# Two up-weight loads moved to ScalarE's queue, the parameter rows moved to SyncE's

## The chip, the cores and the metric

The kernel runs on one core of a Trainium2 chip. Its engines work side by side: TensorE (PE in the profile; its weight loads are shown as PEld), VectorE (DVE), ScalarE (ACT), GpSimd (POOL) and SyncE (SP). Each engine takes its instructions in the order written and waits for others through semaphores. DMA transfers are issued here from the queues of SyncE and of ScalarE; the profile calls the issuing instructions SPq and ACTq. The metric is the time in microseconds (us) of one execution on the device. Less is better.

## The reference

The input x has 2048 rows of 512 numbers. Every row is normalised, and the normalised rows go through two branches that are added to x.

```python
xn = _layernorm(x, axis=-1)
return x + _A_ref(xn, ...) + _B_ref(xn, ...)

def _A_ref(x, Lambda_re, Lambda_im, B_re, B_im, C_re, C_im, log_dt, Dskip):
    dt = jnp.exp(log_dt)
    Lam_bar = jnp.exp(dt * Lam)
    B_bar = ((Lam_bar - 1.0) / Lam)[:, None] * Bmat
    Bu = jnp.einsum("bld,pd->blp", x + 0j, B_bar)
    # for every t: h = Lam_bar * h + Bu[:, t]
    y = 2.0 * jnp.einsum("blp,dp->bld", hseq, Cmat).real + x * Dskip

def _B_ref(x, w_gate, w_up, w_down):
    return (_gelu(x @ w_gate) * (x @ w_up)) @ w_down
```

The first branch is a state space layer with 512 complex states; log_dt, Lambda_re and Lambda_im are its parameter rows, 512 numbers each. The second is a gated feed-forward layer: w_gate and w_up are 512 x 1376, w_down is 1376 x 512. Inputs, weights and the output are bfloat16.

## The kernel before

The 2048 rows are worked in four blocks of 512, and a block is four tiles of 128 rows. For a block the kernel makes the normalised rows, transposes them by DMA so that the 512 features lie on the partitions, multiplies them with the gate and up weights, gates the products, multiplies with the state space input matrix, scans over time on VectorE, and gathers both branches in the output matmuls. TensorE has matmuls of some block to do through nearly the whole run.

The start is arranged differently, and it is the start that the change touches. For block 0 the rows of x are only centred (mean subtracted), transposed on TensorE (`cent_T`, L684) and copied out by ScalarE (L689); the division by the standard deviation is applied to the results. The gate and up products of tiles 0, 1 and 2 over the first 512 hidden columns are built up while the weights arrive: the 512 features are four *steps* k = 0 to 3 of 128, and `GT_k` (L701) adds one step's product to the sum in PSUM. Each step has a load of its own for the gate weights and for the up weights (`ld_wk`, L488, 128 x 512, 128 KB). So TensorE needs, in this order: the gate weights of step 0, the up weights of step 0 (each for tiles 0 and 1), the same for step 1, then gate and up of step 2; then tile 2 catches up on steps 0 to 2, and step 3 closes the sums of all three tiles. After that `GT_mm` (L712) does tile 3 and the columns 512 to 895 of all four tiles, for which the weights come in two larger loads of 384 KB (`ld_w` with slice 1, L493). Two more loads of 480 KB (slice 2, `load_W`) hold the columns from 896 on.

The parameter rows are three loads of 1 KB (`load_par`, L510), each into four rows of a small tile PROW that GpSimd has set to zero (L477). When all three have landed, SyncE issues one DMA transpose of that tile (`tr_par`, L515), which puts the parameters on the partitions. GpSimd's power (L557) and then VectorE's table work (from L558) start from it. On SyncE's queue the transposes of block 0's normalised rows follow (`TR(0)`, L736, four, each waiting for VectorE's L634), then tile loads of block 1 (L482), two long DMA transposes of B_re and B_im (L526), the load of Dskip (L535), x of block 2 (L482), and the transposes of block 1 (`TR(1)`, L736 again), which the matmuls `BU(1)` (L749) read.

What sets the order: a planner inside the kernel. Every operation is written down with an engine, a duration estimated by a formula, and what it reads and writes. For TensorE and SyncE the order is the order in which the operations are written. For ScalarE, VectorE and GpSimd the planner plays the program through with its own durations, and chooses among what is ready by priority. A DMA costs it 0.5 us of the issuing queue, then 2 us plus the bytes at a fixed rate, one transfer after the other. `S.order_behind(op, prev)` pins an operation behind another of the same engine without a semaphore; `GATE["par"]` holds the last DMA of such a chain on ScalarE's queue, and the mean of tile 1 (L956), ScalarE's first computing step, stands behind the chain's end.

The loads at the start go out in this order. SyncE: x tile 0, then for every step its gate and its up weights, with x tile 3 ahead of step 3, then slice 1 of both, slice 2 of both, and tr_par. ScalarE: x tile 1, the three parameter rows, x tile 2.

Of the kernel before, what the change touches and what calls it, by code (L numbers as in the profile page):

```python
# [365 lines left out]
def build(nc, ins, out):  # L366
    with ExitStack() as es:
        E = es.enter_context
        S = Sched(nc, es)
# [9 lines left out]
        WG = A.alloc("WG", [KD, F], BF16)  # L379
        WU = A.alloc("WU", [KD, F], BF16)  # L380
# [4 lines left out]
        WGc = [Buf("WGc%d" % i, "sbx", 10 * i, 10 * i + 1) for i in range(KD + 2)]  # L385
        WUc = [Buf("WUc%d" % i, "sbx", 100 + 10 * i, 101 + 10 * i) for i in range(KD + 2)]
# [34 lines left out]
        PROW = A.alloc("PROW", [128], BF16)  # L421
        PROW16 = Buf("PROW16", "sb", PROW.lo, PROW.hi, PROW.ap[0:16, :])
        PROWq = [Buf("PROW%d" % q, "prow", q, q + 1) for q in range(3)]
# [46 lines left out]
        GATE = {"before_gelu": [], "nh": 0}  # L470
        SCR = A.alloc("SCR", [1], F32)
        half = V(lambda e: e.memset(HALF.ap, 0.5), D_TINY, [], [HALF], "half")
# [10 lines left out]
                X_all.ap[:, 4 * b:4 * b + 4, :], x2[512 * b:512 * (b + 1), :].rearrange("(j p) d -> p j d", p=128)),  # L483
                512 * 1024, writes=X[4 * b:4 * b + 4], tag="ld_x%d" % b)

        def ld_wk(W, Wc, src, k):
            f0, f1 = FC[0]
            return S.dma(lambda e: e.dma_start(W.ap[:, k, f0:f1], src[128 * k:128 * (k + 1), f0:f1]),  # L488
                         256 * (f1 - f0), writes=[Wc[k]], tag="ld_w")

        def ld_w(W, Wc, src, n):
            f0, f1 = FC[n]
            return S.dma(lambda e: e.dma_start(W.ap[:, :, f0:f1], src[:, f0:f1].rearrange("(k p) f -> p k f", p=128)),  # L493
                         1024 * (f1 - f0), writes=[Wc[KD + n - 1]], tag="ld_w")

        def ld_x0(j, queue="sync", after=()):
            return S.dma(lambda e, j=j: e.dma_start(X[j].ap, x2[128 * j:128 * (j + 1), :]), 128 * 1024, writes=[X[j]], tag="ld_x0", queue=queue, after=after)  # L497
        ld_x0(0)
        GATE["par"] = S.order_behind(ld_x0(1, "scalar", [wrm]), GATE["table"])
        for k in range(KD):  # L500
            if k == 3:
                ld_x0(k)
            ld_wk(WG, WGc, ins["B_w_gate"], k)
            ld_wk(WU, WUc, ins["B_w_up"], k)
        ld_w(WG, WGc, ins["B_w_gate"], 1)
        ld_w(WU, WUc, ins["B_w_up"], 1)

        def load_par():
            for q, nm in enumerate(("A_log_dt", "A_Lambda_re", "A_Lambda_im")):
                GATE["par"] = S.order_behind(S.dma(lambda e, q=q, nm=nm: e.dma_start(PROW.ap[4 * q:4 * q + 4, :], ins[nm].rearrange("(s p) -> s p", p=128)),  # L510
                      1024, writes=[PROWq[q]], tag="ld_" + nm, queue="scalar", after=[half]), GATE["par"])
            GATE["par"] = S.order_behind(ld_x0(2, "scalar"), GATE["par"])

        def tr_par():
            S.dma(lambda e: e.dma_start_transpose(PAR.ap.rearrange("p q t -> p (q t)").unsqueeze(1), PROW16.ap), 4096,  # L515
# [434 lines left out]
        def sub(j):  # L950
            return V(lambda e: e.tensor_scalar(XN[j].ap, X[j].ap, MVt[0][j].ap[:, 0:1], None, ALU.subtract),
                     d_dve_ts4x(512), [X[j], MVt[0][j]], [XN[j]], "sub")
        load_par()
        load_W()
        tr_par()
# [103 lines left out]
def bass_parallel_sum__ssm_conv_s5__geglu_ffn__prompt_kernel(  # L1059
    nc: bass.Bass,  # L1060
    A_x: bass.AP,
    A_Lambda_re: bass.AP,
    A_Lambda_im: bass.AP,
    A_B_re: bass.AP,
    A_B_im: bass.AP,
    A_C_re: bass.AP,
    A_C_im: bass.AP,
    A_log_dt: bass.AP,
    A_Dskip: bass.AP,
    B_x: bass.AP,  # L1070
    B_w_gate: bass.AP,
    B_w_up: bass.AP,
    B_w_down: bass.AP,
    out: bass.AP,
):
    ins = {
        "A_x": A_x, "A_Lambda_re": A_Lambda_re, "A_Lambda_im": A_Lambda_im,
        "A_B_re": A_B_re, "A_B_im": A_B_im, "A_C_re": A_C_re, "A_C_im": A_C_im,
        "A_log_dt": A_log_dt, "A_Dskip": A_Dskip,
        "B_w_gate": B_w_gate, "B_w_up": B_w_up, "B_w_down": B_w_down,  # L1080
    }
    build(nc, ins, out)
# [28 lines left out]
```

## Time and profile before

Three runs took 177.21, 176.65 and 176.85 us.

| | us |
|---|---|
| median of the runs | 176.85 |
| the profiled execution | 177.26 |
| its span, first to last instruction | 175.9 |
| TensorE busy | 172.8 (98%) |
| VectorE busy | 159.7 (91%) |
| ScalarE busy | 95.8 (54%) |
| GpSimd busy | 10.7 (6%) |

The granted clock of TensorE is 1.0 in the profiled execution. In the timeline a line gives the start, the duration, the engine, the line of the kernel and the operation, and in brackets how long the engine had been idle before it and what ended that. Several instructions of one kind in a row are merged (x10). "To landing" is the time from the issue of a DMA to its last semaphore update. For the loads of the first microseconds the trace gives:

| load | queue | issued | to landing |
|---|---|---|---|
| x tile 0 | SyncE | 0.74 | 2.1 |
| x tile 1 | ScalarE | 1.00 | 2.2 |
| gate step 0 | SyncE | 1.20 | 2.4 |
| up step 0 | SyncE | 1.66 | 2.9 |
| gate step 1 | SyncE | 2.13 | 3.3 |
| up step 1 | SyncE | 2.60 | 3.7 |
| x tile 2 | ScalarE | 2.66 | 3.4 |
| gate step 2 | SyncE | 3.08 | 3.4 |
| up step 2 | SyncE | 3.56 | 3.6 |
| x tile 3 | SyncE | 4.03 | 3.5 |
| gate step 3 | SyncE | 4.50 | 3.6 |
| up step 3 | SyncE | 4.98 | 3.8 |
| gate slice 1 | SyncE | 5.47 | 4.8 |
| up slice 1 | SyncE | 5.95 | 6.0 |
| gate slice 2 | SyncE | 6.50 | 6.8 |
| up slice 2 | SyncE | 7.04 | 7.6 |
| transpose of the parameters | SyncE | 7.82 | 7.2 |

The parameter rows are issued on ScalarE's queue at 1.42, 2.03 and 2.32; the trace gives no landing for them.

### The profile page before, as it was taken

The numbers are of one execution on the slowest core, as the hardware profiler recorded it, in microseconds if no ns is written. First come the engines' busy times: TensorE is split into PE (matmuls) and PEld (weight loads), VectorE is DVE, ScalarE is ACT, GpSimd is POOL, SyncE is SP. The second block draws the span as 40 slices with busy tenths as digits, with TensorE's granted clock in tenths as the row PEclk, the third lists the DMA queues.
The fourth block names the chain that finished last, engine by engine and source line by source line (L and its number), as shares of the span: only waits on it lengthen the run. The fifth ranks groups of instructions, "written<-read, shape, count | busy, mean of one in ns | idle before, by whom it ended". The sixth has DMA issues, their size and how long they took to land.

```text
span 175.9 us, 2549 instructions
## 1 busy us (share of the span) xinstructions
PE 172.8 (98%) x903; PEld 85.4 (49%) x903; DVE 159.7 (91%) x279; ACT 95.8 (54%) x187; POOL 10.7 (6%) x24
## 2 busy tenths in 40 slices
PE   7999999999999999999999999999999999999995
PEld 2645664744544444444644444444464444444454
DVE  6797999987999989889899999989999899999941
ACT  5367668999766899383676793000667970000000
POOL 3132120211000000002200000000000000000000
DMA  5999989975899000002015000002004000000311
GB/s 144 281 322 154 216 136 203 174 132 114 162 270 270 11 0 2 0 30 75 18 33 112 5 0 4 0 0 89 30 0 34 0 0 0 0 0 4 119 62 60
DMA packets 32421, 14.36 MB, mean 82 GB/s; under 512 B 23737, under 2 KB 32409, under 8 KB 32409
## 3 DMA queue, kind: packets, MB, share of 16 engines
q1 hardware_dynamic: 31952, 13.84, 36.9%
q10 hardware_dynamic: 456, 0.36, 0.6%
q8 instruction: 7, 0.11, 0.3%
q14 instruction: 6, 0.04, 0.1%
HBM read 6.46 MB, written 2.10 MB: 49 GB/s over the span
## 4 chain that ended last, share of the span: by engine, by line
PE 95%; DMA 2%; SPq 1%; issue 0%; DVE 0%
PE PS L885 37%; PE PS L843 32%; PE PS L749 16%; PE PS L712 4%; PE PS L817 3%; PE PS L701 2%; DMA arena<-in_B_w_up_dram 2%; SPq L488 1%; PE PS L684 0%; SPq L497 0%; DVE arena L903 0%
## 5 line engine op out<-in xcount | busy, mean ns | idle before, releaser
L885 PE MATMUL PS<-arena 128*128 128x512 bf16 (+3 forms) x323 | 66.2, 366 | 0.0
L843 PE MATMUL PS<-arena 128*128 128x512 bf16 (+1 forms) x272 | 58.1, 373 | 0.0
L885 PEld LDWEIGHTS PS<-arena 128*128 128x128 bf16 (+1 forms) x323 | 30.8, 98 | 35.2
L843 PEld LDWEIGHTS PS<-arena 128*128 128x128 bf16 x272 | 26.5, 98 | 29.5
L787 DVE TENSOR_TENSOR_SCAN arena<-arena 128x512 bf16<-128x512 f32 x32 | 38.9, 1256 | 0.0
L859 ACT ACTIVATE arena<-PS 128x512 bf16<-128x512 f32 x33 | 19.8, 599 | 26.2 <-DVE arena L903 16.7
L749 PE MATMUL PS<-arena 128*128 128x512 bf16 (+1 forms) x144 | 28.3, 355 | 0.1
L863 ACT ACTIVATE arena<-PS 128x512 bf16<-128x512 f32 x33 | 19.8, 599 | 5.4 <-PE PS L843 5.4
L749 PEld LDWEIGHTS PS<-arena 128*128 128x128 bf16 x144 | 14.0, 98 | 13.7 <-DMA arena<-arena 0.6
L877 ACT ACTIVATE PS<-arena 128x512 f32<-128x512 bf16 (+2 forms) x17 | 9.6, 582 | 19.7 <-DVE arena L903 19.0
L758 ACT ACTIVATE arena<-PS 128x512 bf16<-128x512 f32 x32 | 17.6, 597 | 1.6 <-PE PS L749 1.6
L903 DVE TENSOR_TENSOR arena<-PS,arena 128x512 bf16<-128x512 f32 (+2 forms) x17 | 10.9, 654 | 6.4 <-PE PS L885 6.4
L865 DVE TENSOR_TENSOR arena<-arena 128x512 bf16<-128x512 bf16 x33 | 13.2, 419 | 2.1 <-ACT arena L863 2.0
L776 DVE TENSOR_TENSOR arena<-arena 128x4096 bf16<-128x4096 bf16 (+1 forms) x5 | 9.2, 1859 | 0.4 <-ACT arena L611 0.4
L799 DVE TENSOR_TENSOR arena<-arena 128x4096 bf16<-128x4096 bf16 x4 | 9.2, 2291 | 0.1
L774 DVE TENSOR_TENSOR arena<-arena 128x4096 bf16<-128x4096 bf16 (+1 forms) x5 | 9.2, 1861 | 0.0
L800 DVE TENSOR_TENSOR arena<-arena 128x4096 bf16<-128x4096 bf16 x4 | 9.1, 2287 | 0.0
L615 DVE BATCH_NORM_STATS2 arena<-arena 128x6 f32<-128x512 bf16 x12 | 7.8, 685 | 0.9 <-DMA arena<-in_A_x_dram 0.7
L721 ACT ACTIVATE arena<-PS,arena 128x256 bf16<-128x256 f32 (+1 forms) x16 | 6.5, 450 | 3.3 <-DVE arena L621 1.5
L712 PE MATMUL PS<-arena 128*128 128x512 bf16 (+1 forms) x40 | 7.1, 336 | 0.0
L701 PE MATMUL PS<-arena 128*128 128x256 bf16 (+1 forms) x36 | 6.2, 308 | 0.2 <-DMA arena<-in_B_w_up_dram 0.2
L724 DVE SCALAR_TENSOR_TENSOR arena<-PS,arena 128x256 bf16<-128x256 f32 (+1 forms) x16 | 6.2, 444 | 0.0
(95 smaller groups left out, 124.2 us busy)
## 6 DMA issues: line engine op xcount, KB each, us to landing
out_dram<-arena SPq DMA_DIRECT2D x15, 128.0 KB, 1.7
arena<-in_A_x_dram SPq DMA_DIRECT2D x3, 512.0 KB, 6.3
arena<-in_B_w_down_dram SPq DMA_DIRECT2D x1, 1280.0 KB, 8.8
arena<-in_B_w_gate_dram SPq DMA_DIRECT2D x4, 128.0 KB, 3.4
arena<-in_B_w_up_dram SPq DMA_DIRECT2D x4, 128.0 KB, 3.6
arena<-in_B_w_gate_dram SPq DMA_DIRECT2D x1, 480.0 KB, 6.8
arena<-in_B_w_up_dram SPq DMA_DIRECT2D x1, 480.0 KB, 7.6
arena<-arena SPq DMA_TRANSPOSE x25, 3.3
```

Source lines behind the costliest of these rows:

```text
L701: PE(lambda e: e.matmul(dst, XCd(j, k), WGU[:, ws[0]:ws[-1] + 1, k, f0:f1], start=first, stop=k == KD - 1, skip_group_check=True), d_pe([w ...
L712: ins_ = e.matmul(dst, XCd(j, k), WGU[:, :, k, f0:f1], start=(k == 0), stop=(k == KD - 1))
L749: ins_ = e.matmul(PS[bank][:, 128 * j0:128 * j1], BBT[c][dk].ap[:, 128 * s:128 * (s + 1)], XNT[b].ap[:, dk, 128 * j0:128 * j1], start=(dk ...
L758: GATE["evBu"] = ACT(lambda e, bank=bank, k3=k3, s=s, c=c: e.activation(SSc[k3][s][c].ap, PS[bank][:, :], ACTF.Copy), d_act(512), [BANK[ba ...
L787: V(lambda e, g=g, rb=rb, init=init: e.tensor_tensor_scan(g.ap, rb, g.ap, init, ALU.mult, ALU.add), d_dve_scan(512), [g, PA[RRr]] + ([CARc ...
L843: ins_ = e.matmul(PS[bank][0:m, c0:c1], W.ap[:, dk, 128 * ft:128 * ft + m], XNT[b].ap[:, dk, c0:c1], start=(dk == 0), stop=(dk == KD - 1))
L859: GATE["last_gelu"] = ACT(lambda e, bg=bg, kk=kk, m=m: e.activation(GG[kk].ap[0:m, :], PS[bg][0:m, :], ACTF.Gelu_apprx_tanh), d_act(512), ...
L863: ACT(lambda e, bu=bu, kk=kk, m=m: e.activation(UPB[kk].ap[0:m, :], PS[bu][0:m, :], ACTF.Copy), d_act(512), [BANK[bu]], [UPB[kk]], "evU")
L865: V(lambda e, kk=kk, m=m, ft=ft, k2=k2: e.tensor_tensor(HTt[k2][ft].ap[0:m, :], GG[kk].ap[0:m, :], UPB[kk].ap[0:m, :], ALU.mult), d_dve_tt ...
L877: ACT(lambda e: e.activation(PS[bank][:, c0:c1], X[tt].ap[:, c0:c1], ACTF.Copy), d_act(c1 - c0), [X[tt]], [BANK[bank]], "seed")
L885: ins_ = e.matmul(PS[bank][:, c0:c1], l_[:, 128 * j:128 * (j + 1)], r_[:, c0:c1], start=False, stop=last and n == len(ops) - 1, skip_group ...
L903: V(lambda e: e.tensor_tensor(OUTB[ko].ap[:, c0:c1], PS[bank][:, c0:c1], XD[tt].ap[:, c0:c1], ALU.add), d_dve_1x(c1 - c0), [BANK[bank], XD ...
```

## The change

The up weights of steps 1 and 2 are issued from ScalarE's queue, behind tile 1 of x: step 1's, then tile 2 of x, then step 2's. The three parameter rows leave ScalarE's queue and are issued from SyncE's, behind the up weights of step 3 and ahead of the slice loads. They no longer have a wait on VectorE's first memset written for them (`after=[half]`); the wait on GpSimd's memset of PROW stays, now on SyncE. The mean of tile 1 now stands behind the load of step 2's up weights on ScalarE's queue, where it stood behind that of tile 2.

```diff
-        def ld_wk(W, Wc, src, k):
+        def ld_wk(W, Wc, src, k, queue="sync"):
             f0, f1 = FC[0]
             return S.dma(lambda e: e.dma_start(W.ap[:, k, f0:f1], src[128 * k:128 * (k + 1), f0:f1]),
-                         256 * (f1 - f0), writes=[Wc[k]], tag="ld_w")
+                         256 * (f1 - f0), writes=[Wc[k]], tag="ld_w", queue=queue)
...
             ld_wk(WG, WGc, ins["B_w_gate"], k)
-            ld_wk(WU, WUc, ins["B_w_up"], k)
-        ld_w(WG, WGc, ins["B_w_gate"], 1)
-        ld_w(WU, WUc, ins["B_w_up"], 1)
+            if k in (1, 2):
+                GATE["par"] = S.order_behind(ld_wk(WU, WUc, ins["B_w_up"], k, "scalar"), GATE["par"])
+            else:
+                ld_wk(WU, WUc, ins["B_w_up"], k)
+            if k == 1:
+                GATE["par"] = S.order_behind(ld_x0(2, "scalar"), GATE["par"])
 
         def load_par():
             for q, nm in enumerate(("A_log_dt", "A_Lambda_re", "A_Lambda_im")):
-                GATE["par"] = S.order_behind(S.dma(lambda e, q=q, nm=nm: e.dma_start(PROW.ap[4 * q:4 * q + 4, :], ins[nm].rearrange("(s p) -> s p", p=128)),
-                      1024, writes=[PROWq[q]], tag="ld_" + nm, queue="scalar", after=[half]), GATE["par"])
-            GATE["par"] = S.order_behind(ld_x0(2, "scalar"), GATE["par"])
+                S.dma(lambda e, q=q, nm=nm: e.dma_start(PROW.ap[4 * q:4 * q + 4, :], ins[nm].rearrange("(s p) -> s p", p=128)),
+                      1024, writes=[PROWq[q]], tag="ld_" + nm)
+            ld_w(WG, WGc, ins["B_w_gate"], 1)
+            ld_w(WU, WUc, ins["B_w_up"], 1)
```

## The prediction

> **What bounds the kernel now.** I read the page's chain of work first, then the same chain in order of time, then the timeline of the first 14 us, then the stretches of the first microseconds, and last the timeline of SyncE's queue.
>
> The page's chain, by line:
>
> ```profile
> PE PS L885 37%; PE PS L843 32%; PE PS L749 16%; PE PS L712 4%; PE PS L817 3%; PE PS L701 2%; DMA arena<-in_B_w_up_dram 2%; SPq L488 1%; PE PS L684 0%; SPq L497 0%; DVE arena L903 0%
> ```
>
> TensorE carries 95% of the span. What is not TensorE is one landing of w_up and the issues ahead of it. The chain in order of time (start, duration, what) says where:
>
> ```profile
> 2.60 3.67 DMA arena<-in_B_w_up_dram
> 6.28 0.05 issue
> 6.32 1.26 PE PS L701 x10
> 7.59 0.28 PE PS L684 x4
> 7.86 1.89 PE PS L701 x9
> ...
> 24.61 6.91 PE PS L749 x32
> 31.52 0.12 issue
> 31.64 7.11 PE PS L749 x48
> ```
>
> TensorE waits until 6.28 for the up weights of step 1, issued at 2.60. From 9.7 on it runs without a break but for one at 31.52; after 31.64 there is none. So the time is the instant at which the matmuls at 31.64 start, plus a fixed rest. Two things lead to that instant, and the timeline shows both:
>
> ```profile
> 2.60 0.43 SPq L488 DMA_DIRECT2D arena<-in_B_w_up_dram  x1
> 2.66 0.36 ACTq L497 DMA_DIRECT2D arena<-in_A_x_dram  x1
> ...
> 6.11 0.69 DVE L615 BATCH_NORM_STATS2 arena<-arena 128x6 f32<-128x512 bf16 x1 [0.74 <-DMA arena<-in_A_x_dram]
> 6.32 0.99 PEld L701 LDWEIGHTS PS<-arena 128*128 128x128 bf16 x10 [0.49 <-DMA arena<-in_B_w_up_dram]
> 6.32 1.26 PE L701 MATMUL PS<-arena 128*128 128x256 bf16 x10 [0.21 <-DMA arena<-in_B_w_up_dram]
> ...
> 7.82 1.99 SPq L515 DMA_TRANSPOSE arena<-arena  x1
> ```
>
> First, TensorE itself. The ten matmuls before the wait start at 4.86, one each 0.109 us (a pair takes 0.38, one 0.27), so they have issued by 5.95 and the wait costs 0.37. Two small waits follow the same way, for VectorE's centring of tiles 2 (0.04, before 7.47) and 3 (0.10, before 9.69). VectorE is late because tile 2 of x landed at 6.1 and it idled 0.74 for it.
>
> Second, SyncE's queue, from the wait for tr_par on:
>
> ```profile
> 10.27 5.15 SPq L736 DMA_TRANSPOSE arena<-arena  x4
> 15.46 0.58 SPq L482 DMA_DIRECT2D arena<-in_A_x_dram  x1
> 16.09 3.22 SPq L526 DMA_TRANSPOSE arena<-in_A_B_re_dram  x1
> 19.35 3.67 SPq L526 DMA_TRANSPOSE arena<-in_A_B_im_dram  x1
> 23.07 0.58 SPq L535 DMA_DIRECT2D arena<-in_A_Dskip_dram  x1
> 23.69 0.43 SPq L482 DMA_DIRECT2D arena<-in_A_x_dram  x1
> 24.17 6.34 SPq L736 DMA_TRANSPOSE arena<-arena  x4
> ```
>
> These issues stand back to back from 10.27. The second of the last four (issued 26.62, landed 4.9 later, at 31.5) is what the matmuls at 31.64 need. TensorE was free for them at 24.45 + 32 x 0.216 = 31.36, so 0.28 is lost there. The queue's free-running part begins when the first transpose of block 0 goes out, at 10.27: it waits for VectorE's first normalised tile (the L634 instruction at 9.82, 0.41 long) and stands behind tr_par, which ended at 9.81.
>
> **The change, part by part.** Call p what TensorE gains before 9.7, and s by how much the first transpose of block 0 goes out earlier. The matmuls at 31.64 then start at the later of 31.36 - p and 31.64 - s: the gain is the smaller of p + 0.28 and s, and if s is below zero the loss is s.
>
> ScalarE's queue: the three parameter issues go, two of 128 KB come. Tile 1 stays at 1.00; the up weights of step 1 take the slot at 1.42. Issues of that size there last 0.36 to 0.38 with 0.04 between (the first parameter issue, in that slot, 0.57): tile 2 at 1.83 to 2.04, the up weights of step 2 at 2.24 to 2.45, the end by 2.85. That is 1.18, 0.6 to 0.8 and 1.1 to 1.3 earlier. ScalarE's next work, the mean of tile 1, starts at 3.23 on the landing of tile 1, so the issues lie beside that wait; without this cover they would cost up to 0.38 each.
>
> SyncE's queue: two issues of 0.43 plus 0.04 go. The gate weights of step 2 move up 0.48, tile 3 and both weights of step 3 by 0.95 (the last to 4.03). Three parameter issues follow, each between 0.27 (the Lambda_re issue on ScalarE's queue) and 0.45 (the longest weight issue here); with the gap, 0.93 to 1.47 for three, and I take 1.05, near the small ones. All behind them (four slices of weights, tr_par) is issued 0.1 later (0.0 earlier to 0.5 later). The next weight slices (L493), columns 512 to 895, are covered: the later of the two landed at 11.95, and their first user, the ninth L712 matmul, starts at 12.73.
>
> p: if step 1's up weights land with the 3.7 of their present row, at 5.1, the 0.37 wait is gone; tile 2 at 1.9 + 3.4 = 5.3 closes VectorE's gap (0.74, free at 5.37) and with it the 0.04 and 0.10. p is 0.51. What is late next is the weights of steps 0 and 1 on SyncE's queue: the up weights of step 0 landed at 4.5 and are used at 4.86, the gate weights of step 1 at 5.4 and are used at 5.51. They now share the engines with transfers pulled ahead of them. Lower bound of p: they lose what the others gain, and p is -0.1; I take 0.4.
>
> s has two parts. VectorE's first normalised tile comes 0.6 to 0.74 earlier, at 9.5 to 9.64. tr_par waits for the three parameter rows, and the trace gives their landing nowhere. SyncE reaches tr_par at 7.9. The third row is issued at about 5.2; with the 2.2 that tile 1 took it lands at 7.4, with the 3.8 of step 3's up weights at 9.0. I take 8.0, since it stands directly behind those weights, and they are issued 0.95 earlier than now (present landing 8.8). tr_par lasts 1.99 by its own row, and 1.27 if it were like the transposes of block 1: 9.99, or 9.3. So the first transpose goes out at 10.04 with the former, and s is 0.23; with the latter VectorE sets it, at 9.6, and s is 0.65; with the late landing and 1.99 it goes out at 11.03, and s is -0.76. I keep tr_par's own row: s = 0.23, well under p + 0.28.
>
> The sum goes against the profiled execution, 177.26 (span 175.9 and 1.36 around it), 0.41 above the median of 176.85. Less 0.23 it is 177.0; against the median, 176.6. Under 0.3%, 0.53 us, is what a measurement of this kernel can't tell from nothing.
>
> **Does more queue mean more transfer?** The stretches from 3 to 6 us (busy PE, PEld, DVE, ACT, POOL, clock, DMA share, GB/s):
>
> ```profile
> 3.00:4.50 1.50, 1.36 (x10) 0.43 (x9) 1.24 (x7) 1.21 (x4) 0.00 (x0) 1.00 0.75 197
> 4.50:6.00 1.50, 1.50 (x16) 1.14 (x15) 0.83 (x3) 0.92 (x3) 0.00 (x0) 1.00 1.00 338
> ```
>
> From 4.5 on the DMA engines are full. From 3.0 to 4.5 they are not: at 338 GB/s those 1.5 us would have carried 0.21 MB more, 0.62 us of transfer. That is the stretch in which ScalarE's queue holds the parameter rows and then a late tile 2. So I let step 3's weights land about 0.6 earlier than 8.8, which the 8.0 above rests on. The Trainium skill, page "DMA: Bandwidth & Descriptors", section "Issuing engines are not separate DMA queues", speaks against the change: loads from different engines run on the same 16 DMA engines and only the time to issue is saved. By that rule the 0.6 is not there and the second rival below holds; the 1.00 share agrees with it, the 0.75 leaves room.
>
> **Rivals.**
> 1. Faster by more (26%): tr_par's 1.99 holds some waiting for SyncE's queue to drain, which goes when that queue is shorter; SyncE then waits for VectorE alone, s is 0.65 and p + 0.28 is 0.68 to 0.79: 176.2. For it: SyncE's later transposes last 1.27. Against: the first transpose behind plain loads at 24.17 is long too (6.34 for four).
> 2. Slower (28%): the parameter rows land late. They stand last behind 1.5 MB; if that drains no sooner than now, the third lands at 9.0, tr_par ends at 11.0, and the whole of SyncE's queue to 31 us is 0.76 late, which TensorE waits out at 31.64: 177.6. It decides once the third row lands after 8.24. For it: DMA share 0.93 to 1.00 from 4.5 to 9.0. Against: the room at 3.0 to 4.5.
> 3. A new order (10%): ScalarE's, VectorE's and GpSimd's orders come from the planner's own times, in which the parameter rows and all SyncE transposes are now later. One evacuation put behind a wait such as VectorE's 1.1 for GpSimd at 15.2 eats TensorE's slack (the bank freed at 16.86 is used at 17.93). Either sign; about 0.3 slower, 177.2, and up to 1.
>
> At two queues in turn there is a variant of the low p: the page named above, section "Queues, rings and completion order", has each DMA engine alternate between queue rows, so step 0's up weights would get half the rate. By that rule p is near the -0.1 above, and s still decides; no run here shows it yet.
>
> **How the numbers follow.** Forecast (s from 0.0 to 0.5) 36%, centre 176.6, own range 176.35 to 176.85. Faster by over 0.3%: rival 1 and the upper end of the forecast, 26 + 5 = 31%. Slower: 24 of rival 2's 28 and 9 of rival 3's 10, 33%. Within: the rest, 36%. The range reaches from rival 1's best (p + 0.28 at 0.79, and 0.06 of spread of the runs) at 176.0 to rival 2 at 177.65, and leaves out about 2 in 10.
>
> **What would show it.** Right: step 1's up weights land by 5.3, L701 runs from 4.86 without the 0.21 idle, VectorE's 0.74 gap is gone, tr_par is issued at 8.0 to 8.2, the first L736 on SyncE's queue at about 10.0, and L749 still breaks just before 31.5. Wrong: tr_par starts after 8.5, or waits for w_gate or w_up come up in L701 before 5.6, or the break at L749 is gone and another wait stands behind it.

## The result and the profile after

The changed kernel takes 177.67 us in the median of 7 runs (177.33 to 178.18). The kernel before, timed beside it in 7 runs, takes 176.87 (176.65 to 177.21). The ratio is 1.0039, with a 95% interval of 1.0025 to 1.0054: slower, by 0.4 to 1.0 us. Two later series of the same pair gave 1.0031 (1.0013 to 1.0049) and 1.0034 (1.0022 to 1.0047). All medians below are of the fast runs: four runs of 262 to 473 us, in three of the later series, are left out. The profiled execution took 178.18, the slowest of its series, and its span is 176.9; that of before took 177.26 with a span of 175.9.

On TensorE, VectorE, ScalarE and GpSimd the computing instructions stand in the same order in both programs, so nothing of the difference is a new order. The lines of the code are shifted: L701 of before is L705, L749 is L753, L684 is L688, L615 is L619, L515 is L519, L736 is L740, L510 is L513.

The page of the changed kernel, with the chain by line and the group of the first gate and up products:

```profile
PE PS L889 37%; PE PS L847 32%; PE PS L753 16%; PE PS L716 4%; PE PS L821 3%; DMA arena<-in_B_w_gate_dram 3%; PE PS L705 3%; SPq L488 0%; PE PS L688 0%; SPq L497 0%; DVE arena L907 0%
...
L705 PE MATMUL PS<-arena 128*128 128x256 bf16 (+1 forms) x36 | 6.2, 309 | 1.4 <-DMA arena<-in_B_w_up_dram 0.8
```

Where before had a landing of w_up at 2% of the span, there is now one of w_gate at 3%. The products take the busy time that they took (6.2 us), but 1.4 us of waiting stands ahead of them, where before's L701 had 0.2. The chain in order of time (start, duration, what) says when:

```profile
2.13 5.13 DMA arena<-in_B_w_gate_dram
7.26 0.05 issue
7.31 1.70 PE PS L705 x14
...
25.87 13.85 PE PS L753 x80
```

TensorE waits for the gate weights of step 1, which were issued at 2.13 in both programs. They landed at 7.26, where before they had landed at 5.44. The matmuls of L753 run 80 in a row: the break that L749 had at 31.52 is gone, and not because its transposes came earlier (the second of the four landed at 32.08, in before at 31.55). TensorE is simply later than they are. The timeline, with the idle time ahead of a group in brackets:

```profile
5.84 0.83 PE L705 MATMUL PS<-arena 128*128 128x256 bf16 x6 [0.78 <-DMA arena<-in_B_w_up_dram]
...
7.03 0.69 DVE L619 BATCH_NORM_STATS2 arena<-arena 128x6 f32<-128x512 bf16 x1 [1.62 <-DMA arena<-in_A_x_dram]
...
7.31 1.70 PE L705 MATMUL PS<-arena 128*128 128x256 bf16 x14 [0.63 <-DMA arena<-in_B_w_gate_dram]
...
8.63 1.91 SPq L519 DMA_TRANSPOSE arena<-arena  x1
```

There are two new waits of TensorE. The first ends at 5.84 and is for the up weights of step 0; the second ends at 7.31 and is for the gate weights of step 1. Neither load was touched by the change. Tile 2 of x, which was issued 0.76 earlier, comes later too, and VectorE idles 1.62 for it instead of 0.74. The transpose of the parameters is issued at 8.63 instead of 7.82.

The landings, from the trace, of the loads that matter, with a second trace of before and another of the changed kernel taken later:

| load (needed at, in the first trace of before) | before: issued, landed | before, 2nd trace | after: issued, landed | after, later trace |
|---|---|---|---|---|
| up step 0 (4.86) | 1.66, 4.53 | 4.58 | 1.66, 5.80 | 5.76 |
| gate step 1 (5.51) | 2.13, 5.44 | 5.33 | 2.13, 7.26 | 6.57 |
| up step 1 (5.95) | 2.60, 6.28 | 5.79 | 1.42, 5.36 | 5.57 |
| x tile 2 | 2.66, 6.09 | 5.63 | 1.90, 7.01 | 6.29 |
| up step 2 | 3.56, 7.14 | 6.92 | 2.39, 7.70 | 6.74 |
| up step 3, the last of twelve | 4.98, 8.77 | 8.44 | 4.03, 8.94 | 8.13 |

Of the loads that TensorE needs first, only the up weights of step 1 gained, 0.92 in the first pair of traces and 0.22 in the second. They land 0.2 to 0.4 ahead of the up weights of step 0, which TensorE needs before them and which were issued only 0.24 after them. The twelve loads together are done no earlier or later than the traces of one program differ.

What TensorE loses there is the whole difference. Added up in each trace is by how much the starts of its matmuls lie further apart than back-to-back issue allows, from 4.2 us on. Later gaps of exactly one matmul (0.22), where the trace lacks a record, don't count:

| trace | span | idle of TensorE | span less idle |
|---|---|---|---|
| before | 175.89 | 1.28 | 174.61 |
| before, 2nd | 175.22 | 0.48 | 174.74 |
| after | 176.87 | 2.16 | 174.71 |
| after, later | 176.18 | 1.43 | 174.75 |

The last column hardly moves. The second trace of before lies 0.67 under the first: its up weights of step 1 came at 5.79, before their need, and L749 has no break. So the two waits that the prediction set out to remove, 0.37 and 0.28, are not in every execution. Neither trace is of a middle one: the first is 0.41 above its median, the second, at 176.55, is the fastest of a series with a median of 176.88.

### The profile page after: what moved, and what is told of

Same layout as the page of the kernel before. It is cut to its first block, busy times and chain, and to the rows that moved or that the text cites. A ratio compares the mean times of both kernels' runs of the same rounds, so it can differ in the third digit from the quotient of the medians.

```text
span 176.9 us, 2549 instructions
## 1 busy us (share of the span) xinstructions
PE 172.8 (98%) x903; PEld 85.9 (49%) x903; DVE 159.8 (90%) x279; ACT 95.6 (54%) x187; POOL 10.7 (6%) x24
## 4 chain that ended last, share of the span: by engine, by line
PE 95%; DMA 3%; SPq 1%; DVE 0%; issue 0%
PE PS L889 37%; PE PS L847 32%; PE PS L753 16%; PE PS L716 4%; PE PS L821 3%; DMA arena<-in_B_w_gate_dram 3%; PE PS L705 3%; SPq L488 0%; PE PS L688 0%; SPq L497 0%; DVE arena L907 0%
## 5 line engine op out<-in xcount | busy, mean ns | idle before, releaser
L753 PE MATMUL PS<-arena 128*128 128x512 bf16 (+1 forms) x144 | 28.2, 355 | 0.0
L753 PEld LDWEIGHTS PS<-arena 128*128 128x128 bf16 x144 | 14.1, 98 | 13.4
L619 DVE BATCH_NORM_STATS2 arena<-arena 128x6 f32<-128x512 bf16 x12 | 7.8, 683 | 1.6 <-DMA arena<-in_A_x_dram 1.6
L705 PE MATMUL PS<-arena 128*128 128x256 bf16 (+1 forms) x36 | 6.2, 309 | 1.4 <-DMA arena<-in_B_w_up_dram 0.8
```

Of the source, the lines that this page charges most:

```text
L705: PE(lambda e: e.matmul(dst, XCd(j, k), WGU[:, ws[0]:ws[-1] + 1, k, f0:f1], start=first, stop=k == KD - 1, skip_group_check=True), d_pe([w ...
L753: ins_ = e.matmul(PS[bank][:, 128 * j0:128 * j1], BBT[c][dk].ap[:, 128 * s:128 * (s + 1)], XNT[b].ap[:, dk, 128 * j0:128 * j1], start=(dk ...
```

## The experiments

All comparisons are with the kernel before on the same chip. An edit is shown against the changed kernel unless it says otherwise.

### The halves of the change

**The parameter rows alone.** The up weights go back to SyncE's queue, and tile 2 follows tile 1 on ScalarE's.

```diff
-            if k in (1, 2):
-                GATE["par"] = S.order_behind(ld_wk(WU, WUc, ins["B_w_up"], k, "scalar"), GATE["par"])
-            else:
-                ld_wk(WU, WUc, ins["B_w_up"], k)
+            ld_wk(WU, WUc, ins["B_w_up"], k)
```

> The parameter rows stay on SyncE's queue as in the changed kernel, but the up weights of steps 1 and 2 go back to SyncE's queue; tile 2 of x keeps its early place on ScalarE's queue. Theory of order (the up weights of step 0 and the gate weights of step 1 come late because transfers needed later share the DMA engines with them): only tile 2 is left ahead of them, 128 KB, so step 0's up weights land by about 4.9 and step 1's gate weights by 5.9, L705 waits under 0.6 in all, 176.6 to 177.2. Theory of the parameter rows (the loss comes from tr_par waiting for them and from SyncE's transposes behind it): the third row is issued near 6.1, tr_par goes out at 9.2 or later, the first transpose of block 0 at about 11.2, and the time is 177.5 to 177.9 with no great wait in L705.

Measured: 176.88 against 177.03, ratio 0.9996 (0.9983 to 1.0009). No change. The up weights of step 0 landed at 5.37, later than the 4.9 expected, and the gate weights of step 1 at 5.59; TensorE idles about 0.9 in this trace, between the 0.48 and the 1.28 of before. Its timeline:

```profile
5.41 2.36 PE L702 MATMUL PS<-arena 128*128 128x256 bf16 x20
...
6.14 0.30 SPq L510 DMA_DIRECT2D arena<-in_A_Lambda_im_dram  x1
...
8.67 1.63 SPq L516 DMA_TRANSPOSE arena<-arena  x1
```

The third parameter row is issued at 6.14, later than in the changed kernel (5.21), and the transpose that needs all three starts at 8.67, no earlier than there (8.63). It costs nothing. So the place of the parameter rows isn't the cause, and rival 2's mechanism, though its condition (landing after 8.24) may well hold here, has nothing to bite on. SyncE's queue shows why not:

```profile
23.64 5.48 SPq L737 DMA_TRANSPOSE arena<-arena  x4
```

The first transpose of block 0 went out at 10.35, even a little after the 10.27 of the first trace of before. But the queue behind it is not of a fixed length, as the prediction took it to be. The transpose of B_im took 2.96 here instead of 3.67, so the four transposes of block 1 start at 23.64 instead of 24.17, and they take 5.48, against 6.34 in the first trace of before and 5.46 in the second. The second of the four landed at 30.13 instead of 31.55, and L750 has no break. The break at 31.52 came from those long transposes; it was not set by the start of the queue alone.

**The up weights alone, with the parameter rows on GpSimd's queue.**

```diff
-                      1024, writes=[PROWq[q]], tag="ld_" + nm)
+                      1024, writes=[PROWq[q]], tag="ld_" + nm, queue="gpsimd")
```

> The up weights of steps 1 and 2 and tile 2 on ScalarE's queue as in the changed kernel, but the parameter rows are issued from GpSimd's queue, which is idle then, so that neither SyncE nor ScalarE carries them and tr_par need not wait. Theory of order: as slow as the changed kernel, 177.4 to 177.8, with L705 waiting about 0.9 for step 0's up weights and 0.8 for step 1's gate weights. Theory of the parameter rows: back at the kernel before or better, 176.5 to 176.9.

Measured: 177.84 against 177.03, ratio 1.0048 (1.0032 to 1.0063). Slower, as the whole change is. But only part of that is the kernel's span: the median span is 176.1 against 175.7, and 1.73 us lie outside it where the other kernels have 1.3. Where those 0.4 come from stays open. By the spans alone it loses 0.4, as the changed kernel does in one of its later series (176.1 against 175.7); in the other that loses 0.6. So the up weights don't get clearly cheaper by the parameter rows' leaving SyncE.

**The up weights alone, with the parameter rows on ScalarE's queue behind its first computing steps.** The transpose of the parameters moves behind them.

```diff
+        def ld_par():
+            for q, nm in enumerate(("A_log_dt", "A_Lambda_re", "A_Lambda_im")):
+                GATE["par"] = S.order_behind(S.dma(..., tag="ld_" + nm, queue="scalar"), GATE["par"])
...
         load_W()
-        tr_par()
...                                          # behind the mean of tile 1
+        ld_par()
+        tr_par()
```

> The changed kernel with the parameter rows on ScalarE's queue behind its copies of tile 0 and 1 (issued after about 5), so that SyncE carries none of them and the up weights stay moved. If the moved up weights carry the loss: 0.5 to 0.9 over the kernel before, as the changed kernel. If the parameter rows on SyncE's queue carry it: within 0.2 of the kernel before.

Measured: 178.71 against 177.02, ratio 1.0097 (1.0079 to 1.0115), again with 1.72 outside the span. As a test of the up weights it failed, since the rows came so late that they cost something of their own. In the chain in order of time:

```profile
32.35 0.37 issue
32.72 7.11 PE PS L755 x48
```

and in the timeline of SyncE's queue:

```profile
10.41 1.17 SPq L521 DMA_TRANSPOSE arena<-arena  x1
11.63 5.19 SPq L742 DMA_TRANSPOSE arena<-arena  x4
```

The transpose of the parameters starts at 10.41 and the first of block 0 at 11.63, and now the break ahead of the last 48 matmuls is back. This is much like rival 2, though not all of it is the queue: before the transposes of block 1 go out at 26.09, SyncE has been free since 25.44 and waits for VectorE, which had waited 2.54 for a tile of x. It took the transpose of the parameters at 10.41, some 1.8 us later than in the changed kernel, at least where TensorE itself is late as it is here.

### The order of the loads

**Tile 2 first.** On ScalarE's queue tile 2 stands ahead of both up weights.

```diff
+            if k == 0:
+                ld_wk(WU, WUc, ins["B_w_up"], k)
+                GATE["par"] = S.order_behind(ld_x0(2, "scalar"), GATE["par"])
-            if k in (1, 2):
+            elif k in (1, 2):
                 GATE["par"] = S.order_behind(ld_wk(WU, WUc, ins["B_w_up"], k, "scalar"), GATE["par"])
...
-            if k == 1:
-                GATE["par"] = S.order_behind(ld_x0(2, "scalar"), GATE["par"])
```

> The changed kernel with tile 2 of x ahead of the up weights on ScalarE's queue (tile 1, tile 2, up of step 1, up of step 2). Theory of order: the same bytes are still pulled ahead of step 0's up and step 1's gate weights, TensorE still waits 1.5 to 1.8 us in L705, and although VectorE gets tile 2 about 1.5 us earlier the time stays at 177.3 to 177.7. Rival (VectorE's late tile 2 and with it the late transposes of block 0 carry the loss): 0.5 to 0.8 better than the changed kernel, 176.9 to 177.1.

Measured: 177.29 against 177.03, ratio 1.0016 (1.0004 to 1.0029). Slower than before, by about half as much as the changed kernel, though the intervals overlap. The one execution that was traced was its fastest (176.68) and shows no new stall, so where the others lose isn't seen.

**The order of need.** The up weights of steps 0, 1 and 2 go on ScalarE's queue, the gate weights on SyncE's, with tile 2 behind the gate weights of step 1.

```diff
-            if k in (1, 2):
+            if k < 3:
                 GATE["par"] = S.order_behind(ld_wk(WU, WUc, ins["B_w_up"], k, "scalar"), GATE["par"])
...
             if k == 1:
-                GATE["par"] = S.order_behind(ld_x0(2, "scalar"), GATE["par"])
+                ld_x0(2)
```

> As much on ScalarE's queue as in the changed kernel, but in the order in which TensorE needs it: up weights of steps 0, 1 and 2 behind tile 1; gate weights on SyncE's queue with tile 2 of x between step 1 and step 2. Theory of order: step 0's up weights land by 4.9 and step 1's pair by 6.0, the waits in L705 are at or under those of the kernel before, 176.4 to 177.0. Rival (two queues that both carry weights slow each other whatever the order): waits as in the changed kernel, 177.5 or more. Theory of the parameter rows: they stand where the changed kernel has them, so 177.4 or more.

Measured: 177.31 against 177.03, ratio 1.0022 (1.0007 to 1.0038). The expectation fell: issuing the weights in the order of their need, spread over two queues, is slower than one queue. Its traced execution was the fastest one too (176.97). Step 0's up weights landed at 4.77 in it and the gate weights of step 1 at 4.97, both in time, and TensorE stalls 0.17 at 31.41. The rest of the loss isn't in that trace.

**Tile 2 first, in the kernel before** (an edit of before: tile 2 ahead of the parameter rows).

```diff
         def load_par():
+            GATE["par"] = S.order_behind(ld_x0(2, "scalar"), GATE["par"])
             for q, nm in enumerate(("A_log_dt", "A_Lambda_re", "A_Lambda_im")):
...
-            GATE["par"] = S.order_behind(ld_x0(2, "scalar"), GATE["par"])
```

> The kernel before with one exchange: tile 2 of x ahead of the parameter rows on ScalarE's queue, all weights on SyncE's. Theory of tile 2 (an early tile 2 is what helps, and the changed kernel loses it by putting an up weight ahead of it): tile 2 lands by 5.3, VectorE's gap of 0.74 closes, 0.1 to 0.3 under the kernel before. Theory of sharing: the 128 KB ahead of step 0's up weights cost what tile 2 gains, within 0.15 of the kernel before.

Measured: 177.09 against 177.02, ratio 1.0006 (0.9994 to 1.0018). No change, though tile 2 landed at 4.73, before VectorE needs it. One load pulled ahead on ScalarE's queue can be had for nothing; it brings nothing either.

### How much each load costs

**Spare loads.** The kernel of the first experiment, in which the parameter rows cost nothing, gets two loads of 128 KB more on ScalarE's queue, behind tile 2. They read w_up into memory that nothing uses, so this kernel moves 256 KB that the others don't.

```diff
+                for n in range(2):
+                    GATE["par"] = S.order_behind(S.dma(lambda e, n=n: e.dma_start(TA.ap[:, n, 0, :], ins["B_w_up"][128 * (n + 1):128 * (n + 2), 0:512]),
+                                                       128 * 1024, writes=[...], tag="spare", queue="scalar"), GATE["par"])
```

> The kernel of the first experiment (parameter rows alone moved, tile 2 second on ScalarE's queue) with two loads of 128 KB of w_up more on ScalarE's queue behind tile 2, into memory that is not used yet; all real weights are on SyncE's queue. Theory of sharing: 256 KB more in the engines ahead of the gate and up weights, at about 0.38 per 128 KB, 0.5 to 0.9 over the first experiment, with step 1's weights landing 0.6 later. If the DMA engines had room at 3.0 to 4.5, as the prediction read the share of 0.75: within 0.2 of it.

Measured: 177.68 against 177.02, ratio 1.0035 (1.0022 to 1.0047). That is the slowdown of the change, made by loads that nobody reads, and its timeline shows the same two waits:

```profile
5.69 0.83 PE L705 MATMUL PS<-arena 128*128 128x256 bf16 x6 [0.48 <-DMA arena<-in_B_w_up_dram]
...
6.74 1.94 PE L705 MATMUL PS<-arena 128*128 128x256 bf16 x14 [0.22 <-DMA arena<-in_B_w_gate_dram]
```

Step 1's weights landed 1.1 and 1.2 later than in the trace of the first experiment (gate at 6.70 against 5.59, up at 7.38 against 6.14), twice the 0.6 that was expected. The cause is therefore bytes on the second queue at that time, whatever they are. Two other causes are not needed for it: tile 2 landed in time here (4.70), and ScalarE, which had as many issues to make as in the changed kernel, started its first computing step at 3.42, against 3.35 in the first experiment. Whether the same bytes put forward on SyncE's own queue would cost as much was not run.

**One of the two up weights.** First only step 1's on ScalarE's queue, then only step 2's; the other stays on SyncE's.

```diff
-            if k in (1, 2):
+            if k == 1:      # the second kernel: if k == 2
```

In the second kernel tile 2 is then directly behind tile 1.

> The changed kernel with step 2's up weights back on SyncE's queue: ScalarE's queue holds tile 1, step 1's up weights, tile 2. If the loss comes from step 1's up weights standing ahead of step 0's up weights and of tile 2: nearly all of the changed kernel's loss, 177.3 to 177.6 where the kernel before is at 177.0; step 0's up weights land after 4.9 or tile 2 after 5.4. If each load moved costs about alike: half, 177.2.

> The changed kernel with step 1's up weights back on SyncE's queue: ScalarE's queue holds tile 1, tile 2, step 2's up weights. If the loss comes from step 1's up weights ahead of what is needed first: as the first experiment, 176.8 to 177.1. If each load moved costs about alike, since step 2's up weights share the engines with step 1's gate weights: 177.1 to 177.4.

Measured: 177.19 and 177.31 against 176.95, ratios 1.0013 (1.0004 to 1.0022) and 1.0023 (1.0013 to 1.0034). Each costs something, and 0.13% and 0.23% add to 0.36%, where both together cost 0.31 to 0.39%. In the trace of the first kernel the up weights of step 0 landed at 4.99 and only the gate weights of step 1 come late (6.09, a wait of 0.29). In the second kernel, with only step 2's up weights moved, the timeline has the waits of the changed kernel:

```profile
5.62 0.83 PE L705 MATMUL PS<-arena 128*128 128x256 bf16 x6 [0.49 <-DMA arena<-in_B_w_up_dram]
...
6.69 1.70 PE L705 MATMUL PS<-arena 128*128 128x256 bf16 x14 [0.24 <-DMA arena<-in_B_w_gate_dram]
```

The weights of step 2 are needed after those of steps 0 and 1, and putting them forward delays both (5.57 and 6.64 for up step 0 and gate step 1; with tile 2 alone ahead, in the first experiment, 5.37 and 5.59).

### The same two kernels again

> The changed kernel once more, beside the next three on one chip, for a second look at its start: 0.5 to 0.9 over the kernel before. Theory of sharing: up weights of step 0 or gate weights of step 1 land after their need (4.9 and 5.5) again. Theory of tile 2: tile 2 lands after 6.1 again and the first transpose of block 0 goes out after 10.4.

> The changed kernel beside these two: 0.35 to 0.8 over the kernel before; its trace is one more execution in which the landings of step 0's up weights, step 1's gate weights and tile 2 are read. Theory of sharing: at least one of them after its need (4.9, 5.5, 5.4) again.

> The kernel before, unchanged, for a second trace of it: equal to itself within the interval. If the profiled execution that the prediction was worked from was an ordinary one, TensorE again waits 0.3 to 0.4 for step 1's up weights and 0.2 to 0.3 at L749; if the landings differ by more than 0.3 from execution to execution, these waits differ by as much.

Measured: the changed kernel 177.39 against 177.02 (ratio 1.0031) and 177.55 against 176.95 (ratio 1.0034); the kernel before against itself 176.88 and 176.95, ratio 0.9994 (0.9984 to 1.0005). The trace of the first of these series is of its slowest execution (179.27), which is told of in the last section; up step 0 landed at 5.95 and gate step 1 at 6.62 in it. The timeline of the changed kernel in the second:

```profile
5.81 2.51 PE L705 MATMUL PS<-arena 128*128 128x256 bf16 x20 [0.31 <-DMA arena<-in_B_w_up_dram]
6.31 0.69 DVE L619 BATCH_NORM_STATS2 arena<-arena 128x6 f32<-128x512 bf16 x1 [0.86 <-DMA arena<-in_A_x_dram]
...
8.81 1.18 SPq L519 DMA_TRANSPOSE arena<-arena  x1
10.47 2.54 SPq L740 DMA_TRANSPOSE arena<-arena  x2
```

and that of the kernel before, beside it:

```profile
4.91 2.45 PE L701 MATMUL PS<-arena 128*128 128x256 bf16 x20
5.66 0.69 DVE L615 BATCH_NORM_STATS2 arena<-arena 128x6 f32<-128x512 bf16 x1 [0.24 <-DMA arena<-in_A_x_dram]
...
7.71 2.25 SPq L515 DMA_TRANSPOSE arena<-arena  x1
10.02 2.59 SPq L736 DMA_TRANSPOSE arena<-arena  x2
```

The same 20 matmuls start 0.90 later, behind the up weights of step 0. About 0.3 of that is not their doing: in this execution the matmuls just ahead still start 0.2 apart, until 5.2 us, and in that of before 0.1. SyncE's transposes go out only 0.45 later. The idle times (1.43 and 0.48) differ by 0.95, the spans by 0.96; the medians (177.55 and 176.95) differ by 0.60, since the trace of before is of its fastest execution.

### What they come to

Counted by the loads of 128 KB on ScalarE's queue that are issued between tile 1 and 2.45 us, that is, beside up step 0 and gate step 1 on SyncE's:

| loads ahead | kernel | ratio to before |
|---|---|---|
| 0 | before against itself | 0.9994 |
| 1 (tile 2) | parameter rows alone; tile 2 first in before | 0.9996; 1.0006 |
| 2 | tile 2 with one up weight | 1.0013; 1.0023 |
| 3 | the change, three series; tile 2 with two spare loads | 1.0039, 1.0031, 1.0034; 1.0035 |
| 3, tile 2 first | up weights behind tile 2 | 1.0016 |

By these medians the first load is free and each one after it costs about 0.2 to 0.4 us. Three kernels are not in the table: the order of need (1.0022), where up step 0 is itself among the loads moved, and the two with the parameter rows on other queues, which are longer outside their span.

The traces show what comes in front of the up weights of step 0. When they landed, ScalarE's queue had moved 0.16 and 0.21 MB in the two traces of before, 0.26 and 0.27 with one load ahead, 0.39 in both kernels with two, and 0.46 to 0.50 with three. So most bytes of the three loads move before up step 0 is complete, though two of the three land after it. In the second pair of traces that is 0.28 MB more (0.49 against 0.21). At the 220 to 308 GB/s that the changed kernel's trace shows between 3.0 and 6.0 us it takes 0.9 to 1.3 us, an estimate; up step 0 was 1.18 late (4.58 to 5.76). A single trace can't size a single load: up step 0 landed at 4.91 and 5.37 with one load ahead, at 4.99 and 5.57 with two.

The last row of the table is the one that doesn't fit (4.98, with 0.46 MB moved, at a higher rate), and is left open. No kernel tried is faster than before beyond its interval. TensorE idles 0.48 after 4.2 us in the second trace of before; a middle execution, with a span of 175.6, would idle 0.9 by the same reckoning, so an order of these loads has less than 1 us left to gain.

## Why the prediction was wrong

**The bound: right in place, wrong in how constant it is.** The start did decide, and TensorE's starts plus a fixed rest give the time: the span less the idle is 174.6 to 174.8 in all four traces above. But the 0.37 and 0.28 were taken as properties of the kernel. They were read from an execution 0.4 us above the median, and the second trace, 0.33 below its median, has neither.

**The sum: its form isn't contradicted, both terms are wrong.** It said that the gain is the smaller of p + 0.28 and s. In the second pair of traces, with no break to regain, p is -0.95 (about 0.3 of it from the matmuls that start 0.2 apart) and s is 10.02 - 10.47 = -0.45: the smaller is -0.95, and the span changed by 0.96. So p decided, and s, which the forecast made the limit, didn't bind. The forecast was p = 0.4, s = 0.23. Nor was the path behind s rigid, as the first experiment shows: the same queue reached the transposes of block 1 0.53 earlier from a start 0.08 later.

**The step that failed is the lower bound of p:** "they lose what the others gain, and p is -0.1", and with it "s still decides". (By the prediction's own numbers p + 0.28 would then be 0.18, already under the 0.23 of s.) The prediction named the right loads, up step 0 at 4.86 and gate step 1 at 5.51, and gave them margins of 0.3 and 0.1. It then set the loss at about what the other loads gain, without a sum of the bytes that come in front. Measured, up step 0 landed 1.27 and 1.18 later and gate step 1 1.82 and 1.24 later, which is far beyond the margins, and p was -0.95 in the second pair where 0.4 was forecast and -0.1 the lower bound. Three loads of 0.39, estimated from the 338 GB/s that the prediction quoted, would have given up step 0 at 5.7 (5.80 and 5.76 measured) and p near -0.8. That estimate comes so close partly by luck: fewer bytes came in front (0.28 to 0.30 MB, not 0.39) at a lower rate.

**The reason for that was the room between 3.0 and 4.5 us.** The share of 0.75 was read as time that ScalarE's queue had wasted on parameter rows. The columns are busy PE, PEld, DVE, ACT and POOL, clock, DMA share and GB/s; the changed kernel first:

```profile
3.00:4.50 1.50, 1.50 (x9) 0.49 (x8) 1.24 (x6) 1.01 (x4) 0.00 (x0) 1.00 0.97 206
4.50:6.00 1.50, 0.72 (x8) 0.51 (x9) 0.88 (x3) 1.09 (x3) 0.00 (x0) 1.00 0.93 298
```

and the second trace of before:

```profile
3.00:4.50 1.50, 1.48 (x9) 0.48 (x8) 1.23 (x6) 1.06 (x4) 0.00 (x0) 1.00 0.88 240
```

With the queue filled, the DMA engines were busy (0.97) and moved 206 GB/s, hardly more than the 197 before. And the kernel before moved 240 there in another execution, with the parameter rows where they were. The last of the twelve loads landed at 8.94 and 8.13, against 8.77 and 8.44, though it was issued 0.95 earlier. In none of the three traces of the changed kernel (206, 220 and 218 GB/s) did more issues fill the room. Two other kernels with loads put forward moved 301 and 306 there, one trace each, so what sets the rate of that stretch stays open.

The Trainium skill, page "DMA: Bandwidth & Descriptors", section "Issuing engines are not separate DMA queues", says that loads from different engines run on the same 16 DMA engines and that spreading them saves the issue alone. These landings agree: 0.95 of issue time was saved, and of the landing no more than the traces of one program differ by. The same page, section "Queues, rings and completion order", has each DMA engine take turns between the queue rows. The traces agree as far as they go: when up step 0, third on SyncE's queue, landed in the two traces of the changed kernel, SyncE's queue had moved 0.58 and 0.57 MB and ScalarE's 0.46 and 0.49, near halves, where before it was 0.51 and 0.55 against 0.16 and 0.21. The prediction knew both rules and priced the second at -0.1.

**s and the parameter rows.** The landing of the third row was taken as 8.0; SyncE got past its wait at 8.63 and 8.81, later than the 8.24 from which rival 2 was to decide. Rival 2's sign came true, and its 177.6 lies close to the 177.67 by luck, not by its mechanism: no break stands in L753, and the rows alone cost nothing. The 1.99 of the transpose of the parameters wasn't a fixed length either. It was 1.17 to 2.28 in the traces, and short also when it began as early as before (1.18 from 7.92 on, with tile 2 first). So the 1.99 isn't its own length, as rival 1 supposed. In the eight traces in which it took 1.37 or more it ended 0.04 to 0.42 before the first gate slice landed, whether it had begun at 6.92 or at 8.67. That fits rival 1's wait for the queue to drain, but no run tests it. The changed kernel had nothing from that, since VectorE and TensorE were late by then.

**Tile 2.** It was to land at 5.3 and close VectorE's gap of 0.74. It landed at 7.01 and 6.29, and the gap grew to 1.62 and 0.86. Of the signs that were to show the forecast, the up weights of step 1 by 5.3 nearly came (5.36); of those that were to show it wrong, all came: the transpose after 8.5, a wait for w_up in L705 that began before 5.6, and the break at L749 gone with others in its place.

**Rival 3** is excluded: the order of the computing engines didn't change.

## What to carry to other kernels

The loads at the start are issued faster than they land here, and a second queue added no transfer in the changed kernel: loads that are put forward push back whatever stands beside them, by the bytes that then come in front at the rate that the trace shows. So before putting a load forward, list the loads still in flight that are needed before it, with their margins, and subtract; a share of busy DMA below one in a single execution is not such a margin. And read a wait of a few tenths in two executions before building on it.

## What was unexpected of the hardware

**The rate of the first microseconds differs from execution to execution.** Between 3.0 and 4.5 us the traces show 197 to 306 GB/s, and the share of busy DMA engines doesn't tell which: 0.97 goes with 206, 0.94 with 271. The extremes are the first trace of before (0.75, 197, shown in the prediction) and the kernel with tile 2 first:

```profile
3.00:4.50 1.50, 1.50 (x10) 0.57 (x9) 1.27 (x7) 1.02 (x4) 0.00 (x0) 1.00 1.02 306
```

Why, no run here shows.

**TensorE at half its rate with a granted clock of 1.00.** In one execution of the changed kernel (179.27 us, the slowest of that series) tile 0 of x landed at 4.08 instead of 2.9, and the same 20 matmuls took:

```profile
6.38 3.71 PE L705 MATMUL PS<-arena 128*128 128x256 bf16 x20
```

Elsewhere, where nothing breaks them, they take 2.35 to 2.51. Their starts lie 0.21 apart until 9.2 us and 0.109 from there on, while the row of the clock says 1.00 for that stretch:

```profile
4.40:9.20 4.80, 4.32 (x25) 3.09 (x26) 4.41 (x15) 2.15 (x6) 0.54 (x2) 1.00 1.03 337
```

In the other traces such double distances end between 4.4 and 5.4 us. That a late first tile prolongs them is suggested by this one execution, not shown.
